# Where a vector engine reads its intermediate: halves of a product kept in PSUM instead of SBUF

## The chip, the cores and the metric

The kernel runs on one core of a Trainium2 chip. The metric is the device time of one execution in microseconds (us). Of the core's engines, TensorE (PE in the profile, PEld for its weight loads) multiplies matrices into PSUM, VectorE (DVE), ScalarE (ACT) and GpSimd (POOL) work on the results, and SyncE (SP) issues the DMAs between the chip's large memory (HBM) and the on-chip SBUF. The kernel uses PSUM as eight banks of 512 fp32 numbers per partition; TensorE's results go there, and GpSimd works on SBUF alone in this kernel. Each engine runs its own instructions in the order in which the program has them, and waits on semaphores for the others.

## The reference

Four batches of 12416 tokens with 128 channels pass through an attention over 32 inducing points, and every token's result through a gated feed-forward layer with 1536 hidden units:

```python
def mab(q, kv):
    s = scale * (q @ kv.transpose(0, 2, 1))
    s = s - s.max(-1, keepdims=True)
    a = np.exp(s)
    a /= a.sum(-1, keepdims=True) + 1e-09
    return a @ kv
h = mab(I, x)            # 32 points attend to all tokens of the batch
attn = mab(x, h)         # every token attends to the 32 points

g = attn @ w_gate
silu = g * (1.0 / (1.0 + np.exp(-g)))
val = attn @ w_val
out = (silu * val) @ w_out
```

x, the inducing points and the weights are fp32, and so is the output.

## The kernel before, in words

**Feed-forward.** The second attention is never multiplied out: gate and value weights are first multiplied by the batch's 32 points (st.w), and the tokens' attention weights (a stack of high and low halves) are the other operand. A batch is 25 *columns* of 512 or 480 tokens: one of 512 for the first blocks, then twelve of 512 and twelve of 480. Each column has 12 *tiles* of 128 hidden units. Batch 0 goes tile by tile in fp32r; batches 1 to 3 go by *pairs* of tiles in fp16, each fp32 number as a high half (its 16-bit cast) and a low half (the rest). A *slot* is one tile, so a column has 12 slots and a batch 300. For a pair the work is:

- fronts (L894): four matmuls, gate and value of two tiles, into two PSUM tiles gw of two banks each; three such tiles exist
- gates (L908): ScalarE makes silu of the gate, 2 x 512 or 2 x 480 numbers per partition
- values (L912): VectorE multiplies value, a factor and silu into h, in SBUF (5 buffers)
- splits, one pair later: h_hi is the cast of h to 16 bits (L916), h_lo = h - h_hi (L917). ScalarE casts, except tiles 6 and 7, which VectorE casts, and in batch 3 also tile 11; GpSimd subtracts, except tiles 2 and 3, which VectorE subtracts
- back (L934 to L936), 8 to 14 tiles later: three matmuls per tile, w_lo x h_hi, w_hi x h_hi and w_hi x h_lo, summed over the column's 12 tiles in one PSUM bank o; there are two such banks
- at the column's end VectorE scales o into SBUF (ob, L944), and a DMA writes it out

**Attention.** While batch b passes through the feed-forward layer, the attention of batch b + 1 is computed in small steps between its slots: scores (s1), two bursts of exp (e1 and e2), sums over tokens (hacc), the points and factors that scale them by powers of two (h_a to h_c, size_a to size_d), the tokens' scores (s2, s2_max, s2_sub), and the product with the weights (proj). The row sums and their reciprocals (sum2, rec2), normalization, transposes and halves (norm2, aT, a_hi, a_lo) follow during the batch itself, for four columns at a time. Steps that need a PSUM bank borrow the o bank that is not collecting a column.

**What sets the order.** The program is written out in order. plan() gives every attention step a slot, with numbers in PA (for batch 0) and PB (for batches 1 and 2); a step runs when the loop reaches its slot, but steps marked acc are held while the next back tile is 11, 0 or 1. Within a slot pair each engine gets, in this order, its part of fronts, gates and values of the new pair, splits of the pair before, backs, and attention steps. In batch 0, peak_of, peak_a, peak_b and peak_c find the largest weights, and half_a, half_b and half_c make the 16-bit halves of w_out; WPK and WOH are the slots where they start.

Of the kernel before, what the change touches and what calls it, by code (L numbers as in the profile page):

```python
# [110 lines left out]
@with_exitstack
def induced_set_attention_then_swiglu(ctx: ExitStack, tc: tile.TileContext, xt, xn, ind, wgv, wo, out):
# [104 lines left out]
    def peak_b():  # L217
        peaks = keep[-1]
        ps = ps_o.tile([P, 512], F32, name="o")
        for k in range(2):  # L220
# [4 lines left out]
        inverse2(top[:, 2:3], top[:, 1:2])

    def peak_c():
        nc.vector.tensor_scalar(out=top[:, 2:3], in0=top[:, 2:3], scalar1=2.0 ** TOP, scalar2=None, op0=ALU.mult)
# [73 lines left out]
    def attention(b, one, xn0=None, xt0=None):  # L302
# [209 lines left out]
        def size_b():
            ps = ps_o.tile([P, 512], F32, name="o")
            nc.tensor.matmul(out=ps[:, 0:M], lhsT=ones, rhs=st.size, start=True, stop=True)
# [15 lines left out]

# [76 lines left out]
        def rec2(q):  # L607
            nc.vector.reciprocal(out=st.sm[q][:, :FC[q]], in_=st.sm[q][:, :FC[q]])
            if st.half:
                nc.vector.tensor_mul(out=st.sm[q][:, :FC[q]], in0=st.sm[q][:, :FC[q]], in1=powers[:, 0:1].broadcast_to([P, FC[q]]))  # L610

# [285 lines left out]

    def on(u, two_, eng, call):

        if u.last or two_[0] != two_[1]:  # L900
            for k in range(2):
                call(eng[two_[k]], lambda x: x[:, k])
        else:
            call(eng[two_[0]], lambda x: x)

    def gates(u):
        u.s = twin(sip.tile([P, 2 * WF], F32, name="silu"), u)
        on(u, (0, 0), (nc.scalar,), lambda e, f: e.activation(out=f(u.s), in_=f(u.g), func=AF.Silu, scale=u.st.g))  # L908

    def values(u):  # L910
        u.h = twin(hp.tile([P, 2 * WF], F32, name="h"), u)
        on(u, (0, 0), (nc.vector,), lambda e, f: e.scalar_tensor_tensor(out=f(u.h), in0=f(u.v), scalar=u.st.k, in1=f(u.s), op0=ALU.mult, op1=ALU.mult))  # L912

    def splits(u):
        u.hi, u.lo = [twin(p.tile([P, WB], F32R, name=name).bitcast(F16)[:, :2 * WF], u) for p, name in ((hip, "h_hi"), (lop, "h_lo"))]
        on(u, [x.t in CAST2[u.b == B - 1] or u.cast_dve for x in u.us], (nc.scalar.copy, nc.vector.tensor_copy), lambda e, f: e(out=f(u.hi), in_=f(u.h)))  # L916
        on(u, [x.t in SUB2 or (u.last and x is u) for x in u.us], (nc.gpsimd, nc.vector), lambda e, f: e.tensor_sub(out=f(u.lo), in0=f(u.h), in1=f(u.hi)))  # L917
# [50 lines left out]
    for b in range(B):  # L968
        nxt = attention(b + 1, (one, oneb)[(b + 1) % 2]) if b + 1 < B else None
        if nxt is not None:  # L970
            nxt.steps = plan(nxt, PA if b == 0 else PB)
            if b == 0:
                cur.steps.append((nxt.e1, lambda: run(f"e2:52:{NTB}")))
                for q in range(2, NF):
                    base = NT * (1 + NG * (q - 1) - NST) + 2
# [2 lines left out]
                once = [lambda x=(k, i): peak_of(*x) for k in range(2) for i in range((6, 3)[k])] + [peak_a, lambda: None, peak_b, lambda: None, peak_c]
                peak_b.acc = (8, 9, 10, 11, 0, 1)
                cur.steps += [(WPK + 4 * i, f) for i, f in enumerate(once)]  # L980
                cur.steps += [(WOH + 4 * i, lambda i=i: (half_a, half_b, half_c)[i % 3](i // 3)) for i in range(9)]
# [95 lines left out]
```

## Time and profile before

| | us |
|---|---|
| median of 3 runs (lowest, highest) | 1488.93 (1487.92, 1491.02) |
| the profiled execution: time | 1488.93 |
| its span | 1487.2 |
| outside the span | 1.7 |

The mean granted TensorE clock was 0.995 of full speed. Column outputs (L944, and L946 in batch 0) begin where one column is summed up, so they cut the span: batch 0's last one begins at 421.70 us, batch 1's at 785.46, batch 2's at 1145.05, and batch 3's last but one at 1474.09.

A group line of the profile names the line, the engine, the operation, written and read tiles, shapes and the count, then busy us and the mean ns of one, then idle time before it and who ended it. A line of waits names who waited for whom, the total, the number and the longest. A line of the chain or of a timeline begins with the start and the duration. Durations of neighbours on one engine can overlap a little at their ends. In shapes, 128x960 and 128x2x480 are the same pair of 480-token tiles.

### The profile page before, as it was taken

To read this page: it belongs to the slowest core of one execution; us is meant where nothing else is said; L and a number is where in the kernel's file an instruction comes from. 1 tells how busy PE (TensorE), PEld (TensorE's weight loads), DVE (VectorE), ACT (ScalarE), POOL (GpSimd) and SP (SyncE) were. 2 spreads that over 40 slices of the span, in tenths; PEclk is the share of its full clock that TensorE was granted. 3 is DMA by queue.
4 is the path that set the end of the run, shared out by engine and by line. 5 is a ranking of instruction groups with operands and counts; after the bars stand their busy time and mean duration, and the time that the engine had idled before them with its cause. 6 is when DMAs were issued, how large, how long until landed. Compare 5 with 4: busy or idle time off the path is not lost.

```text
span 1487.2 us, 22279 instructions
## 1 busy us (share of the span) xinstructions
PE 1413.7 (95%) x7462; PEld 772.3 (52%) x7462; DVE 1276.4 (86%) x1572; ACT 1183.5 (80%) x1492; POOL 1175.7 (79%) x708
## 2 busy tenths in 40 slices
PE   8999999999999999999999998999999999999898
PEld 5677777788844443444444444344444344344443
DVE  6889878987888889688888887878888999999998
ACT  5887798799987876788888786688888787777786
POOL 1698769888978768688888776868888888888887
PEclk9999999999999999999999999999999999999999
DMA  9234422211124222110022431210001001000000
GB/s 369 64 99 154 141 72 94 104 48 48 43 91 164 80 101 96 37 39 29 30 81 78 172 101 47 100 43 31 30 29 34 29 26 32 22 32 31 28 24 26
DMA packets 50803, 107.75 MB, mean 72 GB/s; under 512 B 12928, under 2 KB 32896, under 8 KB 50688
## 3 DMA queue, kind: packets, MB, share of 16 engines
q1 hardware_dynamic: 50688, 106.33, 21.3%
q8 instruction: 59, 0.97, 0.3%
q14 instruction: 56, 0.46, 0.1%
HBM read 62.87 MB, written 25.43 MB: 59 GB/s over the span
## 4 chain that ended last, share of the span: by engine, by line
PE 63%; DVE 11%; ACT 10%; issue 6%; POOL 6%; DMA 3%; SPq 1%; POOLq 0%; DVEq 0%; ACTq 0%
PE gw L894 16%; PE o L936 12%; PE o L934 11%; PE o L935 11%; DVE h L912 6%; POOL h_lo L917 5%; ACT silu L908 5%; PE gv L854 4%; PE gv L853 4%; ACT h_hi L916 2%; ACT silu L859 1%; DVE h_lo L917 1%; PE o L436 1%; ACT h_hi L875 1%; DMA s_all<-wgv 1%
## 5 line engine op out<-in xcount | busy, mean ns | idle before, releaser
L917 POOL TENSOR_TENSOR h_lo<-h,h_hi 128x1024 f16<-128x1024 f32 (+1 forms) x375 | 796.9, 2147 | 204.5 <-ACT h_hi L916 84.2
L912 DVE SCALAR_TENSOR_TENSOR h<-gw,sc,silu 128x1024 f32<-128x1024 f32 (+1 forms) x451 | 558.0, 1241 | 122.3 <-ACT silu L908 108.1
L908 ACT ACTIVATE silu<-gw,sc 128x1024 f32<-128x1024 f32 (+1 forms) x451 | 489.8, 1087 | 181.5 <-PE gw L894 125.3
L916 ACT CAST h_hi<-h 128x1024 f16<-128x1024 f32 (+3 forms) x371 | 365.4, 985 | 36.5 <-DVE h L912 33.2
L936 PE MATMUL o<-h_lo,work 128*128 128x512 f16 (+1 forms) x900 | 336.7, 374 | 13.2 <-POOL h_lo L917 13.1
L935 PE MATMUL o<-h_hi,work 128*128 128x512 f16 (+1 forms) x900 | 337.0, 374 | 0.0
L934 PE MATMUL o<-h_hi,work 128*128 128x512 f16 (+1 forms) x900 | 336.7, 374 | 0.0
L894 PE MATMUL gw<-stack,work 128*128 128x512 f16 (+1 forms) x1200 | 302.0, 373 | 24.8 <-DVE h L912 19.0
L877 POOL TENSOR_TENSOR h_lo<-h,h_hi 128x512 fp32r<-128x512 f32 (+1 forms) x216 | 270.1, 1274 | 59.7 <-ACT h_hi L875 34.3
L894 PEld LDWEIGHTS <-work 128*128 128x128 f16 x1200 | 116.4, 98 | 170.6 <-issue 44.9
L859 ACT ACTIVATE silu<-gv 128x512 f32<-128x512 f32 (+1 forms) x300 | 176.3, 589 | 31.3 <-PE gv L853 24.8
L867 DVE TENSOR_TENSOR h<-gv,silu 128x512 f32<-128x512 f32 (+1 forms) x216 | 143.1, 667 | 38.3 <-ACT silu L859 24.5
L894 PE MATMUL gw<-stack,tw 128*128 128x512 f16 (+1 forms) x600 | 151.3, 374 | 9.9 <-DVE h L912 6.3
L934 PEld LDWEIGHTS <-work 128*128 128x128 f16 x900 | 88.4, 98 | 120.5 <-issue 24.2
L936 PEld LDWEIGHTS <-work 128*128 128x128 f16 x900 | 88.2, 98 | 101.1 <-issue 1.1
L935 PEld LDWEIGHTS <-work 128*128 128x128 f16 x900 | 88.1, 98 | 100.1 <-issue 1.0
L917 DVE TENSOR_TENSOR h_lo<-h,h_hi 128x1024 f16<-128x1024 f32 (+1 forms) x76 | 137.4, 1808 | 0.0
L875 ACT CAST h_hi<-h 128x512 fp32r<-128x512 f32 (+1 forms) x190 | 115.1, 606 | 14.9 <-DVE h L867 13.3
L853 PE MATMUL gv<-stack,tw 128*128 128x512 f32 (+1 forms) x300 | 120.5, 402 | 2.3 <-DVE stack L695 1.2
L854 PE MATMUL gv<-stack,tw 128*128 128x512 f32 (+1 forms) x300 | 117.0, 390 | 0.7 <-ACT silu L859 0.4
L934 PE MATMUL o<-h_hi,wo_lo 128*128 128x512 f32 (+1 forms) x288 | 112.8, 392 | 0.0
L935 PE MATMUL o<-h_hi,wo_hi 128*128 128x512 f32 (+1 forms) x288 | 111.4, 387 | 0.0
(216 smaller groups left out, 1386.3 us busy)
## 6 DMA issues: line engine op xcount, KB each, us to landing
xt_sb<-xt SPq DMA_DIRECT2D x32, 896.0 KB, 5.3
xn_sb<-xn SPq DMA_DIRECT2D x18, 896.0 KB, 6.7
out<-ob SPq DMA_DIRECT2D x52, 256.0 KB, 2.0
out<-ob SPq DMA_DIRECT2D x48, 240.0 KB, 2.0
xt_sb<-xt SPq DMA_DIRECT2D x4, 832.0 KB, 4.8
xn_sb<-xn SPq DMA_DIRECT2D x3, 832.0 KB, 4.6
stack<-a_hi SPq DMA_DIRECT2D x72, 32.0 KB, 1.8
stack<-a_lo SPq DMA_DIRECT2D x72, 32.0 KB, 1.9
```

The source lines that it names most:

```text
L853: nc.tensor.matmul(out=u.g[:, :n], lhsT=st.w[:, wcol(0, t)], rhs=rhs, start=True, stop=True)
L854: nc.tensor.matmul(out=u.v[:, :n], lhsT=st.w[:, wcol(1, t)], rhs=rhs, start=True, stop=True)
L859: nc.scalar.activation(out=u.s[:, :u.n], in_=u.g[:, :u.n], func=AF.Silu)
L877: eng.tensor_sub(out=u.lo[:, :n], in0=u.h[:, :n], in1=u.hi[:, :n].bitcast(F32))
L894: nc.tensor.matmul(out=x[:, 512 * (u.t - t):][:, :u.n], lhsT=st.w[:, wcol(k, u.t)], rhs=st.stack[c][:, :u.n], start=True, stop=True)
L908: on(u, (0, 0), (nc.scalar,), lambda e, f: e.activation(out=f(u.s), in_=f(u.g), func=AF.Silu, scale=u.st.g))
L912: on(u, (0, 0), (nc.vector,), lambda e, f: e.scalar_tensor_tensor(out=f(u.h), in0=f(u.v), scalar=u.st.k, in1=f(u.s), op0=ALU.mult, op1=ALU ...
L916: on(u, [x.t in CAST2[u.b == B - 1] or u.cast_dve for x in u.us], (nc.scalar.copy, nc.vector.tensor_copy), lambda e, f: e(out=f(u.hi), in_ ...
L917: on(u, [x.t in SUB2 or (u.last and x is u) for x in u.us], (nc.gpsimd, nc.vector), lambda e, f: e.tensor_sub(out=f(u.lo), in0=f(u.h), in1 ...
L934: nc.tensor.matmul(out=o[:, :n], lhsT=w_lo[:, ws], rhs=u.hi[:, :n], start=(t == 0), stop=False)
L935: nc.tensor.matmul(out=o[:, :n], lhsT=w_hi[:, ws], rhs=u.hi[:, :n], start=False, stop=False)
L936: nc.tensor.matmul(out=o[:, :n], lhsT=w_hi[:, ws], rhs=u.lo[:, :n], start=False, stop=(t == NT - 1))
```

## The change

Four things are changed.

1. **Owned pairs.** A pair can be *owned*: then its two tiles are handled apart. The product of the first goes to SBUF as before, and that of the second into the o bank that is not collecting (u.x). ScalarE casts and GpSimd subtracts the first half; VectorE casts and subtracts the second, from PSUM. A pair is owned when the next back tile is one of 1 to 6, no burst is due, no step marked acc is due within 5 slots or has run in the last 8, and the pair owned before lies at least two pairs back. The fixed choice of tiles (SUB2, CAST2) goes: pairs that are not owned are cast by ScalarE and subtracted by GpSimd. In a burst VectorE casts with a reduction over an axis of length one (one_wide). Of the 450 pairs 114 become owned: two per column in batch 3 (one in its last), two per column in most of batches 1 and 2, and one or none in columns 2 to 11 of these, where the next batch's attention runs.
2. **Small operations.** size_a takes absolute values with a reduction; size_b keeps its intermediates in PSUM; size_c, size_d and the factor in rec2 go from VectorE to ScalarE.
3. **Slots.** The size steps stand 2, 8, 12 and 16 slots after h_c instead of 2, 5, 8 and 11, and HB in PB begins 2 slots later.
4. **Batch 0.** The peak steps begin at slot 84, 3 apart (before: 66, 4 apart), with peak_a at 112, peak_b at 120 and the rest after the first burst; half_a to half_c begin at 216, 8 apart (before: 136, 4 apart), and their sum lies in an h buffer.

```diff
-SUB2, CAST2 = {2, 3}, ({6, 7}, {6, 7, 11})
-WPK, WOH = 66, 136
+OWN = range(1, 7)
+REST = 2
+WPK, WPA, WOH = 84, 112, 216
...
-PB = dict(... HB=(9, 3), ...)
+PB = dict(... HB=(11, 3), ...)
...
 def half_a(i):
-        joint[i] = sgl.tile([P, WF], F32, name="aT")
+        joint[i] = hp.tile([P, 2 * WF], F32, name="h")[:, :WF]
...
 def size_a():
-            nc.vector.tensor_scalar(out=st.size.bitcast(U32), in0=st.hT[:, 0:M].bitcast(U32), scalar1=0x7FFFFFFF, scalar2=None, op0=ALU.bitwise_and)
+            nc.vector.tensor_reduce(out=st.size, in_=st.hT[:, 0:M].unsqueeze(2), op=ALU.max, axis=AX.X, apply_absolute_value=True)
...
+        def grow(out, in_, by):
+            nc.scalar.activation(out=out, in_=in_, func=AF.Copy, scale=by)
+
 def size_c():
-            nc.vector.tensor_scalar(out=st.sc[:, 0:2], in0=powers[:, 0:2], scalar1=st.sc[:, 6:7], scalar2=None, op0=ALU.mult)
+            grow(st.sc[:, 0:2], powers[:, 0:2], st.sc[:, 6:7])
...
 def rec2(q):
-                nc.vector.tensor_mul(out=st.sm[q][:, :FC[q]], in0=st.sm[q][:, :FC[q]], in1=powers[:, 0:1].broadcast_to([P, FC[q]]))
+                nc.scalar.activation(out=st.sm[q][:, :FC[q]], in_=st.sm[q][:, :FC[q]], func=AF.Copy, scale=2.0 ** TOP)
...
-            add(hn + 3 * i + 2, step)
+            add(hn + (2, 8, 12, 16)[i], step)
...
+    halves = (lambda x: x[:, 0], lambda x: x[:, 1])
+    whole = (lambda x: x,)
...
 def values(u):
         u.h = twin(hp.tile([P, 2 * WF], F32, name="h"), u)
-        on(u, (0, 0), (nc.vector,), lambda e, f: e.scalar_tensor_tensor(out=f(u.h), in0=f(u.v), scalar=u.st.k, in1=f(u.s), op0=ALU.mult, op1=ALU.mult))
+        u.x = ps_o.tile([P, 512], F32, name="o")[:, :u.n] if u.own else None
+        u.parts = [(f, u.x if u.own and f is halves[1] else f(u.h)) for f in (halves if u.own else whole)]
+        for f, h in u.parts:
+            nc.vector.scalar_tensor_tensor(out=h, in0=f(u.v), scalar=u.st.k, in1=f(u.s), op0=ALU.mult, op1=ALU.mult)
+
+    def one_wide(out, in_):
+        nc.vector.tensor_reduce(out=out, in_=in_.unsqueeze(len(in_.shape)), op=ALU.max, axis=AX.X)

 def splits(u):
-        on(u, [x.t in CAST2[u.b == B - 1] or u.cast_dve for x in u.us], (nc.scalar.copy, nc.vector.tensor_copy), lambda e, f: e(out=f(u.hi), in_=f(u.h)))
-        on(u, [x.t in SUB2 or (u.last and x is u) for x in u.us], (nc.gpsimd, nc.vector), lambda e, f: e.tensor_sub(out=f(u.lo), in0=f(u.h), in1=f(u.hi)))
+        for f, h in u.parts:
+            (nc.vector.tensor_copy if h is u.x else one_wide if u.cast_dve else nc.scalar.copy)(out=f(u.hi), in_=h)
+        for f, h in u.parts:
+            (nc.vector if h is u.x else nc.gpsimd).tensor_sub(out=f(u.lo), in0=h, in1=f(u.hi))
...
+    quiet = {"own": 0, "step": 0}
+
+    def owned(slot, burst):
+
+        soon = [f for a in (cur, nxt) if a is not None for at, f in a.steps if at <= slot + 5]
+        ok = not burst and pend and pend[0].t in OWN and slot >= max(quiet.values()) and not any(hasattr(f, "acc") and f.acc for f in soon)
+        if ok:
+            quiet["own"] = slot + 2 * REST
+        return ok
...
+                cur.steps += [(WPK + 3 * i, f) for i, f in enumerate(once)]
+                cur.steps += [(WPA, peak_a), (WPA + 8, peak_b), (nxt.e1 + 9, peak_c), (nxt.e1 + 13, peak_d)]
+                cur.steps += [(WOH + 8 * i, lambda i=i: (half_a, half_b, half_c)[i % 3](i // 3)) for i in range(9)]
...
                 u.cast_dve = burst
+                u.own = u.last or owned(slot2, burst)
...
+                        if getattr(a.steps[0][1], "acc", ()):
+                            quiet["step"] = slot + 8
```

More of the change, by code (lines that the diff above doesn't have):

```diff
@@ L225, in peak_b, with peak_d @@
         inverse2(top[:, 2:3], top[:, 1:2])
-    def peak_c():
+    def peak_d():
         nc.vector.tensor_scalar(out=top[:, 2:3], in0=top[:, 2:3], scalar1=2.0 ** TOP, scalar2=None, op0=ALU.mult)
@@ L517, in size_b @@
             st.up, st.k, st.g, st.u, st.low = [c(i) for i in range(5)]
-            nc.vector.tensor_reduce(out=c(5), in_=ps[:, 0:M], op=ALU.max, axis=AX.X)
-            nc.vector.tensor_scalar(out=c(5), in0=c(5), scalar1=top[:, 0:1], scalar2=TINY, op0=ALU.mult, op1=ALU.max)
-            floor2(st.low, c(5))
+            nc.vector.tensor_reduce(out=ps[:, 64:65], in_=ps[:, 0:M], op=ALU.max, axis=AX.X)
+            nc.vector.tensor_scalar(out=ps[:, 65:66], in0=ps[:, 64:65], scalar1=top[:, 0:1], scalar2=TINY, op0=ALU.mult, op1=ALU.max)
+            floor2(st.low, ps[:, 65:66])
             inverse2(c(6), st.low)
+        def grow(out, in_, by):
+            nc.scalar.activation(out=out, in_=in_, func=AF.Copy, scale=by)
         def size_c():
-            nc.vector.tensor_scalar(out=st.sc[:, 0:2], in0=powers[:, 0:2], scalar1=st.sc[:, 6:7], scalar2=None, op0=ALU.mult)
-            nc.vector.tensor_scalar(out=st.sc[:, 2:4], in0=powers[:, 2:4], scalar1=st.low, scalar2=None, op0=ALU.mult)
-            nc.vector.tensor_mul(out=st.u, in0=st.u, in1=st.low)
+            grow(st.sc[:, 0:2], powers[:, 0:2], st.sc[:, 6:7])
+            grow(st.sc[:, 2:4], powers[:, 2:4], st.low)
+            grow(st.u, st.u, st.low)
         def size_d():
-            nc.vector.tensor_scalar(out=st.hT[:, 0:M], in0=st.hT[:, 0:M], scalar1=st.up, scalar2=None, op0=ALU.mult)
+            grow(st.hT[:, 0:M], st.hT[:, 0:M], st.up)
         def weights():
@@ L896, in fronts @@
         return u
[L898 to L904, printed above, removed]
+    halves = (lambda x: x[:, 0], lambda x: x[:, 1])
+    whole = (lambda x: x,)
     def gates(u):
         u.s = twin(sip.tile([P, 2 * WF], F32, name="silu"), u)
-        on(u, (0, 0), (nc.scalar,), lambda e, f: e.activation(out=f(u.s), in_=f(u.g), func=AF.Silu, scale=u.st.g))
+        for f in halves if u.last else whole:
+            nc.scalar.activation(out=f(u.s), in_=f(u.g), func=AF.Silu, scale=u.st.g)
     def values(u):
         u.h = twin(hp.tile([P, 2 * WF], F32, name="h"), u)
-        on(u, (0, 0), (nc.vector,), lambda e, f: e.scalar_tensor_tensor(out=f(u.h), in0=f(u.v), scalar=u.st.k, in1=f(u.s), op0=ALU.mult, op1=ALU.mult))
+        u.x = ps_o.tile([P, 512], F32, name="o")[:, :u.n] if u.own else None
[4 more added lines that the diff above has]
+        nc.vector.tensor_reduce(out=out, in_=in_.unsqueeze(len(in_.shape)), op=ALU.max, axis=AX.X)
     def splits(u):
         u.hi, u.lo = [twin(p.tile([P, WB], F32R, name=name).bitcast(F16)[:, :2 * WF], u) for p, name in ((hip, "h_hi"), (lop, "h_lo"))]
-        on(u, [x.t in CAST2[u.b == B - 1] or u.cast_dve for x in u.us], (nc.scalar.copy, nc.vector.tensor_copy), lambda e, f: e(out=f(u.hi), in_=f(u.h)))
-        on(u, [x.t in SUB2 or (u.last and x is u) for x in u.us], (nc.gpsimd, nc.vector), lambda e, f: e.tensor_sub(out=f(u.lo), in0=f(u.h), in1=f(u.hi)))
+        for f, h in u.parts:
+            (nc.vector.tensor_copy if h is u.x else one_wide if u.cast_dve else nc.scalar.copy)(out=f(u.hi), in_=h)
+        for f, h in u.parts:
+            (nc.vector if h is u.x else nc.gpsimd).tensor_sub(out=f(u.lo), in0=h, in1=f(u.hi))
         for k, x in enumerate(u.us):
@@ L977, in induced_set_attention_then_swiglu @@
                     cur.steps += post(cur, q, nc.gpsimd, base)
[L978 to L981, printed above, removed]
+                once = [lambda x=(k, i): peak_of(*x) for k in range(2) for i in range((6, 3)[k])]
+                cur.steps += [(WPK + 3 * i, f) for i, f in enumerate(once)]
+                cur.steps += [(WPA, peak_a), (WPA + 8, peak_b), (nxt.e1 + 9, peak_c), (nxt.e1 + 13, peak_d)]
+                peak_b.acc = (NT - 1, 0, 1)
+                cur.steps += [(WOH + 8 * i, lambda i=i: (half_a, half_b, half_c)[i % 3](i // 3)) for i in range(9)]
                 cur.steps.sort(key=lambda x: x[0])
@@ L1031, in induced_set_attention_then_swiglu @@
                     steps(slot)
+        quiet = {k: at - SLOTS for k, at in quiet.items()}
         if nxt is not None:
```

3 lines of the change are left out of this document (2 added, 1 removed).

## The prediction

> **What bounds the kernel now.** I read the page's busy line first, then the busy time in six stretches, then PE's pace in the chain of waits, then who waits for whom in batch 3.
>
> ```profile
> PE 1413.7 (95%) x7462; PEld 772.3 (52%) x7462; DVE 1276.4 (86%) x1572; ACT 1183.5 (80%) x1492; POOL 1175.7 (79%) x708
> ```
>
> 95% of PE says little here, because consecutive matmuls overlap in the records. The stretches below start and end at the start of a column's output copy (L944); they hold 11, 12, 11, 12, 12 and 11 columns. The columns are PE, PEld, DVE, ACT and POOL busy, clock, DMA share, GB/s.
>
> ```profile
> 441.14:614.17 173.03, 163.14 (x974) 72.06 (x972) 144.51 (x174) 128.99 (x127) 130.16 (x68) 0.99 0.29 100
> 614.17:768.58 154.41, 149.45 (x724) 70.59 (x723) 131.18 (x133) 129.27 (x133) 131.24 (x68) 1.00 0.11 34
> 800.28:977.12 176.84, 165.96 (x980) 73.66 (x979) 144.87 (x174) 129.63 (x128) 128.98 (x68) 0.98 0.29 98
> 977.12:1131.34 154.22, 149.18 (x723) 70.45 (x722) 131.29 (x133) 129.27 (x133) 131.36 (x68) 1.00 0.11 35
> 1158.82:1326.92 168.10, 157.46 (x715) 69.67 (x714) 159.96 (x139) 131.00 (x132) 138.20 (x66) 1.00 0.09 29
> 1326.92:1474.09 147.17, 137.93 (x668) 65.02 (x667) 139.83 (x123) 115.81 (x122) 122.73 (x61) 1.00 0.08 27
> ```
>
> Batch 3 (last two rows) is VectorE's: 160.0 of 168.1 us and 139.8 of 147.2 us, 95% in both, at 14.01 us for a 512-token column and 13.38 us for a 480-token one. The second halves of batches 1 and 2 take 12.87 and 12.85 us for the same 480 tokens, with VectorE at 85%. The chain shows what PE does when it waits for nothing: it passes one group of four gate and value matmuls (one pair of tiles) per period. First and last of five groups at 512 tokens, and of nine at 480:
>
> ```profile
> 1191.35 0.86 PE gw L894 x4
> ...
> 1199.99 0.86 PE gw L894 x4
> ```
> ```profile
> 657.92 0.81 PE gw L894 x4
> ...
> 674.12 0.81 PE gw L894 x4
> ```
>
> 8.64 us over 4 periods is 2.16 us a pair, and 16.20 over 8 is 2.025; six pairs make PE's own pace 12.95 us (512) and 12.15 us (480) a column. Above it lie 12.7 us in batch 3's 512-token columns (168.10 - 12 x 12.95), 13.5 us in its 480-token ones, 8.6 and 8.4 us in the second halves of batches 1 and 2. No more than these 43 us is to be had there. Who holds PE up in batch 3 (us in total, times, longest):
>
> ```profile
> PE gw L894 <- DVE h L912: 12.9, 12, 1.8
> PE o L936 <- POOL h_lo L917: 5.6, 11, 0.8
> ```
>
> And why VectorE is that full: VectorE, then GpSimd, in one column of batch 3.
>
> ```profile
> 1203.88 0.68 DVE L916 CAST h_hi<-h 128x1024 f16<-128x1024 f32 x1
> 1207.36 1.89 DVE L916 CAST h_hi<-h 128x512 f16<-128x512 f32 x1
> 1211.73 2.99 DVE L917 TENSOR_TENSOR h_lo<-h,h_hi 128x1024 f16<-128x1024 f32 x1
> ```
> ```profile
> 1204.73 4.23 POOL L917 TENSOR_TENSOR h_lo<-h,h_hi 128x1024 f16<-128x1024 f32 x2 [1.82 <-DVE h_hi L916]
> 1209.42 7.29 POOL L917 TENSOR_TENSOR h_lo<-h,h_hi 128x1024 f16<-128x1024 f32 x3 [0.46 <-DVE h_hi L916]
> ```
>
> A cast of half the size takes 1.89 us instead of 0.68. It starts while GpSimd subtracts and ends at 1209.25, 0.3 us behind GpSimd's pair (1208.96). The 2.99 us subtraction likewise lies inside GpSimd's next three, which take 7.29 us where the pair before took 2 x 2.12. With h in SBUF the two engines take turns. The Trainium skill (SBUF — State Buffer, "SBUF: two separate sides") has a rule for it: VectorE and GpSimd share one pair of ports, locked for a whole instruction, and the loser waits; these rows agree.
>
> **The change, part by part.** Prices, from groups of one line and shape (count, busy us, mean ns):
>
> ```profile
> L912 DVE SCALAR_TENSOR_TENSOR h<-gw,sc,silu 128x960 f32<-128x960 f32 x215 | 258.9, 1208 | 51.9 <-ACT silu L908 44.8 <-POOL h_lo L917 5.4
> L917 DVE TENSOR_TENSOR h_lo<-h,h_hi 128x960 f16<-128x960 f32 x36 | 66.9, 1859 | 0.0
> L916 DVE CAST h_hi<-h 128x960 f16<-128x960 f32 x36 | 31.1, 863 | 0.0
> L916 DVE CAST h_hi<-h 128x480 f16<-128x480 f32 x12 | 18.5, 1542 | 0.0
> L877 DVE TENSOR_TENSOR h_lo<-gv,h_hi 128x480 fp32r<-128x480 f32 x36 | 23.4, 649 | 0.1
> L867 DVE TENSOR_TENSOR gv<-gv,silu 128x480 f32<-128x480 f32 x36 | 23.8, 660 | 3.1 <-ACT silu L859 3.0
> L946 DVE COPY ob<-o 128x480 f32<-128x480 f32 x12 | 7.8, 647 | 0.0
> L917 POOL TENSOR_TENSOR h_lo<-h,h_hi 128x960 f16<-128x960 f32 x179 | 370.5, 2093 | 70.5 <-DVE h_hi L916 32.4 <-PE gw L894 17.0 <-ACT h_hi L916 14.8
> L877 POOL TENSOR_TENSOR h_lo<-h,h_hi 128x480 fp32r<-128x480 f32 x108 | 130.7, 1234 | 24.6 <-ACT h_hi L875 11.6 <-DVE h_hi L875 8.5 <-PE o L935 2.4
> L916 ACT CAST h_hi<-h 128x960 f16<-128x960 f32 x168 | 165.5, 985 | 16.6 <-DVE h L912 15.6
> L916 ACT CAST h_hi<-h 128x480 f16<-128x480 f32 x12 | 7.0, 584 | 0.7 <-DVE h L912 0.7
> ```
>
> The last two columns of the run hold the one half-size product and the last subtraction:
>
> ```profile
> L912 DVE SCALAR_TENSOR_TENSOR h<-gw,sc,silu 128x480 f32<-128x480 f32 x2 | 1.3, 703 | 0.0
> L917 DVE TENSOR_TENSOR h_lo<-h,h_hi 128x480 f16<-128x480 f32 x1 | 2.3, 2341 | 0.0
> ```
>
> *VectorE, batch 3, 480 tokens.* Out go one subtraction (1.86), one whole cast (0.86) and one half cast (1.54): 4.26 us. In come, for two owned pairs, two more product instructions (2 x 0.703 - 1.208 = 0.20 a pair), two casts from PSUM and two subtractions from PSUM. The subtraction from PSUM has its row, 0.65 (batch 0, where GpSimd is as busy). The product into PSUM has a relative, 0.66 in place in PSUM, beside 0.70 for a half in SBUF; I take 0.70. The cast from PSUM to 16 bits has none; it is nearest to the PSUM copy, 0.65, its ends being 0.43 (half of the SBUF cast's 0.863) and 1.54 (the half cast that waits). So 2 x (0.20 + 0.65 + 0.65) = 3.0 us in, and VectorE's 12.71 us a column (139.83/11) become 11.4. The skill has a rule against this (VectorE: DVE Perf Modes, "Why PSUM operands drop a tier"): an fp32 operand in PSUM loses the copy's double rate. By it the cast is 0.65; with the double rate it would be 0.43 and VectorE at 11.0.
>
> *ScalarE* gains half a cast in such a column: out 4 x 0.985 + 0.584, in 4 x 0.985 + 2 x 0.584, so 10.53 us (115.81/11) become 11.1. It also takes over a small multiplication behind the row sums, once in four columns, from VectorE:
>
> ```profile
> L610 DVE TENSOR_TENSOR sm<-sm,powers 128x15 f32<-128x15 f32 x9 | 11.5, 1273 | 0.3
> L294 DVE TENSOR_REDUCE pairs<-s_all 128x15 f32<-128x480 f32 x12 | 7.7, 643 | 0.0
> ```
>
> 1.27 us for 15 numbers a row, twice the reduction of 480, is again a wait for the port. On ScalarE it adds a wait instead: it follows the reciprocal, which stands behind a product (1.21) and that reduction (0.64), while ScalarE has only a cast (0.985) to do. So ScalarE stands still for some 1 us, 0.25 us a column, with the next pair's silu behind it and PE's next gate matmuls behind that. I put it inside the 0.25 that I add below. *GpSimd* gives one subtraction (2.09) for two halves between 1.05 and 1.23, I take 1.15: 11.16 becomes 11.4. All three then stand under PE's 12.15, at 91 to 94%, and none waits for a shared port. What is late next is PE itself. I add 0.25 us a column for what three engines at 94% still do to it (between 0 and the 0.72 that batch 1 shows): 12.4, and 13.2 at 512 tokens, where all scale alike.
>
> The order of VectorE's work in one 480-token column of batch 3, before, and then after (h, h_hi, h_lo: product, its 16-bit half, the rest; o: an output bank of PSUM):
>
> ```order
> L944 TENSOR_SCALAR ob<-o,sc 128x480
> L912 SCALAR_TENSOR_TENSOR h<-gw,sc,silu 128x2x480
> L916 CAST h_hi<-h 128x2x480
> L912 SCALAR_TENSOR_TENSOR h<-gw,sc,silu 128x2x480 x2
> L916 CAST h_hi<-h 128x480
> L912 SCALAR_TENSOR_TENSOR h<-gw,sc,silu 128x2x480 x2
> L917 TENSOR_TENSOR h_lo<-h,h_hi 128x2x480
> L912 SCALAR_TENSOR_TENSOR h<-gw,sc,silu 128x2x480
> ```
> ```order
> L954 TENSOR_SCALAR ob<-o,sc 128x480
> L917 SCALAR_TENSOR_TENSOR h<-gw,sc,silu 128x2x480
> L917 SCALAR_TENSOR_TENSOR h<-gw,sc,silu 128x480
> L917 SCALAR_TENSOR_TENSOR o<-gw,sc,silu 128x480
> L917 SCALAR_TENSOR_TENSOR h<-gw,sc,silu 128x2x480
> L925 CAST h_hi<-o 128x480
> L927 TENSOR_TENSOR h_lo<-o,h_hi 128x480
> L917 SCALAR_TENSOR_TENSOR h<-gw,sc,silu 128x480
> L917 SCALAR_TENSOR_TENSOR o<-gw,sc,silu 128x480
> ```
>
> No row of the second touches h in SBUF except to write it. The bank is read out one pair after it is taken, and it is taken only while the column's output stands between its tiles 1 and 6, so the next column's first output matmul finds it free and PE gains no wait. If not, PE waits for one subtraction, 0.65 us a column, as much as (b) below.
>
> *The sum.* Batch 3: 12 x (14.01 - 13.2) = 9.7 and 11 x (13.38 - 12.4) = 10.8. Its last pair loses a 2.34 us subtraction for one of 0.65: 1.5. Batches 1 and 2, second halves: 12 x 0.47 + 12 x 0.45 = 11.0.
>
> *Batches 1 and 2, columns 1 to 11,* hold the next batch's attention. From column 4 on hardly any pair is owned, so VectorE drops its cast and its subtraction, and each column gives GpSimd and ScalarE a sixth of both. PE's waits there in batch 1, and ScalarE's largest on GpSimd:
>
> ```profile
> PE gw L894 <- ACT silu L908: 2.4, 1, 2.4
> PE o L436 <- DMA xn_sb<-xn: 2.1, 1, 2.1
> PE o L363 <- DVE s_all L586: 1.8, 1, 1.8
> PE gw L894 <- DVE h L912: 1.3, 3, 0.6
> PE o L363 <- DVE s_all L398: 0.8, 1, 0.8
> PE o L514 <- DVE ob L944: 0.8, 1, 0.8
> ```
> ```profile
> ACT s_all L601 <- POOL s_all L598: 3.6, 1, 3.6
> ```
>
> The four of VectorE are 4.7 us; I take 3.5 as gained in each batch, 7. The DMA's wait stays, as the load it waits for moves by the same two slots as its reader. GpSimd's order up to the second exp, before and after (s_all<-s_all,mx: the maximum taken off the scores; the exp waits for the last of seven):
>
> ```order
> L203 TENSOR_TENSOR sc<-wide,sc 128x1
> L917 TENSOR_TENSOR h_lo<-h,h_hi 128x1024 x5
> L614 TENSOR_TENSOR s_all<-s_all,sm 128x480
> L917 TENSOR_TENSOR h_lo<-h,h_hi 128x1024 x2
> L598 TENSOR_TENSOR s_all<-s_all,mx2a 128x448
> ```
> ```order
> L204 TENSOR_TENSOR sc<-wide,sc 128x1
> L927 TENSOR_TENSOR h_lo<-h,h_hi 128x1024 x4
> L620 TENSOR_TENSOR s_all<-s_all,sm 128x480
> L927 TENSOR_TENSOR h_lo<-h,h_hi 128x1024 x3
> L604 TENSOR_TENSOR s_all<-s_all,mx2a 128x448
> ```
>
> The first row comes three slots later than before, so equal counts behind it mean one or two more subtractions ahead of the exp, up to 2 x 2.1 us. GpSimd loses its port waits in return. Ends: 14 us gained over both batches (all of VectorE's waits and ScalarE's 2.4), 8.6 lost. The small factors moved to ScalarE are hidden under its idle time. *Batch 0:* the weight peaks and the joined weights are only spread out, 1 us, between -4 and 4.
>
> 9.7 + 10.8 + 1.5 + 11.0 + 7 + 1 = 41 us, off the profiled execution's 1488.93 (span 1487.2), which is also the median: **1448 us**, with an own range of 1439 to 1460 (PE's pace plus 0.05 to plus 0.5 us in the 47 columns).
>
> **Rivals.** (a) *PE's pace, nothing left over.* If the shared port made all the waiting, columns run at 12.95 and 12.15: 12.7 + 13.5 + 1.5 + 17.0 + 7 + 1 = 53, 1436 us. The skill's lock rule would have it so. Against: three engines near 94% seldom fit without loss. (b) *ScalarE and GpSimd, in series, keep today's loss.* Batch 3 comes only to batch 1's 0.72 us above PE: 12 x 0.34 + 11 x 0.51 + 1.5 = 11 us, 1478. For: batch 1 loses 0.72 with VectorE at 85%. Against: it still has one locked subtraction a column. (c) *GpSimd late before the exp:* the 7 becomes -8.6, 1464. (d) *Slower: VectorE at PSUM is dearer than its rows.* If each owned pair costs e more, a 480-token column takes 11.4 + 2e on VectorE; it decides from e = 0.5, and at e = 1.0 batch 3 is where it was. At e = 1.3 (cast and subtraction doubled) it is 14.0: 11 x 0.6 + 12 x 0.9 + 24 x 1.1 = 44 us lost less 7, 1526. For: no row shows a 16-bit cast out of PSUM. Against: the 0.65 and 0.66 rows. (e) The columns don't move, 1488.
>
> **Chances.** Forecast 0.50, (a) 0.17, (b) 0.13, (c) 0.12, (d) 0.05, (e) 0.03. (a) to (c) and the forecast are faster: 0.92; within 0.2% (3 us, about what a measurement of this kernel tells from no change) 0.03; slower 0.05. The range 1433 to 1477 takes in (a), (c) and nearly (b).
>
> **What would show it.** Right: half casts and subtractions on VectorE near 0.65 us with no long tail, GpSimd's whole 512-token subtractions at 2.12 us with few above, batch 3 columns near 13.2 and 12.4, PE's wait on h under 4 us there. Wrong: PE waiting for GpSimd's h_lo instead, ScalarE waiting longer than 3.6 us before the second exp, or VectorE still at 95% of batch 3.

## The result, and the profile after

The changed kernel takes 1445.88 us (median; 1444.28 to 1446.7) against 1488.93 before: a ratio of 0.9707, 95% interval 0.9693 to 0.9721. The forecast was 1448. The profiled execution took 1444.72 us, its span 1442.9. The total is right; how it comes about is only half right, as the terms below show.

Busy time of the kernel after, from its page:

```profile
PE 1398.7 (97%) x7462; PEld 770.0 (53%) x7462; DVE 1184.9 (82%) x1704; ACT 1213.6 (84%) x1600; POOL 1186.1 (82%) x783
```

VectorE has 132 more instructions and 91.5 us less to do. The six stretches that the prediction showed of before, cut at the same columns (PE, PEld, DVE, ACT, POOL busy, clock, DMA share, GB/s). The cuts, there and here, lie 0.23 us ahead of the output starts that a timeline shows, all alike, so the lengths between them hold:

```profile
436.77:604.78 168.01, 160.92 (x974) 71.79 (x973) 124.45 (x158) 136.84 (x144) 142.02 (x78) 1.00 0.30 103
604.78:757.60 152.82, 148.33 (x725) 70.53 (x724) 131.56 (x177) 131.18 (x150) 129.50 (x81) 1.00 0.12 35
787.21:956.99 169.78, 161.96 (x979) 72.31 (x978) 124.55 (x158) 137.15 (x144) 141.93 (x77) 1.00 0.29 101
956.99:1109.81 152.82, 148.31 (x725) 70.54 (x724) 131.57 (x177) 131.10 (x150) 129.56 (x81) 1.00 0.12 35
1135.14:1294.37 159.23, 155.81 (x721) 70.23 (x720) 136.98 (x172) 136.64 (x148) 134.81 (x79) 1.00 0.10 30
1294.37:1431.19 136.82, 134.40 (x663) 64.48 (x662) 117.94 (x154) 119.40 (x135) 116.06 (x71) 1.00 0.09 29
```

Batch 3 is down from 168.10 to 159.23 and from 147.17 to 136.82, to 13.27 and 12.44 us a column (forecast 13.2 and 12.4), with all three engines at 85 to 87%. The second halves of batches 1 and 2 went from 154.41 and 154.22 only to 152.82 and 152.82, where 148.8 was forecast.

The prices, from groups of one line and shape (count, busy us, mean ns, idle before):

```profile
L917 DVE SCALAR_TENSOR_TENSOR o<-gw,sc,silu 128x480 f32<-128x480 f32 x72 | 51.6, 716 | 0.0
L925 DVE CAST h_hi<-o 128x480 f16<-128x480 f32 x72 | 46.6, 648 | 0.0
L927 DVE TENSOR_TENSOR h_lo<-o,h_hi 128x480 f16<-128x480 f32 x72 | 47.3, 658 | 2.5
L925 DVE CAST h_hi<-o 128x512 f16<-128x512 f32 x42 | 28.6, 680 | 0.0
L927 DVE TENSOR_TENSOR h_lo<-o,h_hi 128x512 f16<-128x512 f32 x42 | 29.0, 691 | 1.5
L927 POOL TENSOR_TENSOR h_lo<-h,h_hi 128x1024 f16<-128x1024 f32 x192 | 408.1, 2135 | 78.9 <-ACT h_hi L925 76.9
L927 POOL TENSOR_TENSOR h_lo<-h,h_hi 128x480 f16<-128x480 f32 x72 | 79.2, 1100 | 15.6 <-ACT h_hi L925 15.6
```

Cast and subtraction from PSUM take 0.65 and 0.66 us, as forecast, where a half cast from SBUF had taken 1.54 before. Who waits in batch 3 (us in total, times, longest):

```profile
ACT sm L616 <- DVE sm L614: 10.2, 5, 2.1
PE gw L900 <- ACT silu L910: 5.8, 5, 1.2
```

PE no longer waits for VectorE there (12.9 us before) nor for GpSimd (5.6). Its only wait there is new: five times, once per set of row sums, it waits for ScalarE's silu. Such a place, ScalarE, VectorE and PE in the timeline of one 480-token column of batch 3 (start, duration; the idle time before and its cause in brackets):

```profile
1351.28 0.98 ACT L925 CAST h_hi<-h 128x960 f16<-128x960 f32 x1
1354.28 0.21 ACT L616 ACTIVATE sm<-sm 128x15 f32<-128x15 f32 x1 [2.02 <-DVE sm L614]
1354.40 1.04 ACT L910 ACTIVATE silu<-gw,sc 128x960 f32<-128x960 f32 x1
```
```profile
1350.59 0.65 DVE L925 CAST h_hi<-o 128x480 f16<-128x480 f32 x1
1351.27 0.66 DVE L927 TENSOR_TENSOR h_lo<-o,h_hi 128x480 f16<-128x480 f32 x1
1351.85 0.71 DVE L917 SCALAR_TENSOR_TENSOR h<-gw,sc,silu 128x480 f32<-128x480 f32 x1
1352.47 0.72 DVE L917 SCALAR_TENSOR_TENSOR o<-gw,sc,silu 128x480 f32<-128x480 f32 x1
1353.10 0.64 DVE L297 TENSOR_REDUCE pairs<-s_all 128x15 f32<-128x480 f32 x1
1353.78 0.18 DVE L298 TENSOR_REDUCE sm<-pairs 128x15 f32<-128x30 f32 x1
1353.99 0.25 DVE L614 RECIPROCAL sm<-sm 128x15 f32<-128x15 f32 x1
```
```profile
1355.49 0.56 PE L900 MATMUL gw<-stack,work 128*128 128x480 f16 x2 [1.21 <-ACT silu L910]
```

ScalarE has cast a pair and stands for 2.02 us until VectorE has done these seven instructions, to multiply 15 numbers in 0.21 us; the silu behind that releases PE 1.21 us late. The starts of the column outputs show the loss:

```profile
1332.72 0.71 DVE L954 TENSOR_SCALAR ob<-o,sc 128x480 f32<-128x480 f32 x1
1344.87 0.71 DVE L954 TENSOR_SCALAR ob<-o,sc 128x480 f32<-128x480 f32 x1
1359.05 0.71 DVE L954 TENSOR_SCALAR ob<-o,sc 128x480 f32<-128x480 f32 x1
1370.68 0.71 DVE L954 TENSOR_SCALAR ob<-o,sc 128x480 f32<-128x480 f32 x1
```

A column without row sums takes 12.15 us, PE's pace. That with the row sums and the next, 14.18 + 11.63 = 25.81 us, are 1.51 over two at that pace (24.30).

### The profile page after: what moved, and what is told of

Same layout as the page of the kernel before. It is cut to its first block, busy times and chain, and to the rows that moved or that the text cites. A ratio compares the mean times of both kernels' runs of the same rounds, so it can differ in the third digit from the quotient of the medians.

```text
span 1442.9 us, 22347 instructions
## 1 busy us (share of the span) xinstructions
PE 1398.7 (97%) x7462; PEld 770.0 (53%) x7462; DVE 1184.9 (82%) x1704; ACT 1213.6 (84%) x1600; POOL 1186.1 (82%) x783
## 5 line engine op out<-in xcount | busy, mean ns | idle before, releaser
L927 POOL TENSOR_TENSOR h_lo<-h,h_hi 128x1024 f16<-128x1024 f32 (+2 forms) x450 | 821.4, 1840 | 154.2 <-ACT h_hi L925 151.2
L917 DVE SCALAR_TENSOR_TENSOR h<-gw,sc,silu 128x1024 f32<-128x1024 f32 (+2 forms) x450 | 502.1, 1117 | 163.8 <-ACT silu L910 151.6
L925 ACT CAST h_hi<-h 128x1024 f16<-128x1024 f32 (+3 forms) x446 | 404.3, 907 | 14.0 <-DVE h L917 13.4
L900 PE MATMUL gw<-stack,work 128*128 128x512 f16 (+1 forms) x1200 | 303.6, 373 | 18.1 <-ACT silu L910 16.5
L900 PE MATMUL gw<-stack,tw 128*128 128x512 f16 (+1 forms) x600 | 152.4, 373 | 10.6 <-ACT silu L910 9.6
L946 PE MATMUL o<-h_lo,wo_hi 128*128 128x512 f32 (+1 forms) x288 | 111.3, 387 | 0.1
```

The source lines that it names most:

```text
L900: nc.tensor.matmul(out=x[:, 512 * (u.t - t):][:, :u.n], lhsT=st.w[:, wcol(k, u.t)], rhs=st.stack[c][:, :u.n], start=True, stop=True)
L917: nc.vector.scalar_tensor_tensor(out=h, in0=f(u.v), scalar=u.st.k, in1=f(u.s), op0=ALU.mult, op1=ALU.mult)
L925: (nc.vector.tensor_copy if h is u.x else one_wide if u.cast_dve else nc.scalar.copy)(out=f(u.hi), in_=h)
L927: (nc.vector if h is u.x else nc.gpsimd).tensor_sub(out=f(u.lo), in0=h, in1=f(u.hi))
L946: nc.tensor.matmul(out=o[:, :n], lhsT=w_hi[:, ws], rhs=u.lo[:, :n], start=False, stop=(t == NT - 1))
```

## The experiments

Times are medians; ratios are to the kernel before, run beside each (1488.77 to 1489.05 us). "Stretch" means the six of above, in their order.

**The owned half back in SBUF.** The work stays the same, instruction for instruction; only the place of the second half differs.

```diff
-        u.x = ps_o.tile([P, 512], F32, name="o")[:, :u.n] if u.own else None
+        u.x = halves[1](u.h) if u.own else None
```

> The changed kernel with one thing undone: the second half of an owned pair stays in SBUF, in the upper half of its h tile. Engines, sizes and order are those of the changed kernel; only the place differs. Theory 'port' (VectorE and GpSimd take turns when VectorE reads h from SBUF, and that is where the time went): VectorE's half casts go from 0.65 us to about 1.5, its half subtractions from 0.66 to about 1.6, so each owned pair costs it some 1.8 us more; a 480-token column of batch 3 needs 11.0 + 3.6 = 14.6 us on VectorE instead of 12.4, and the whole 1490 to 1535 us, no better than before the change. Theory 'load' (the gain is that work was divided better among the engines): 1446 us, within 5.

1481.6 us, ratio 0.9949 (0.9932 to 0.9966): 36 of the 43 us are lost again by the place alone.

```profile
L925 DVE CAST h_hi<-h 128x480 f16<-128x480 f32 x72 | 71.0, 986 | 0.0
L927 DVE TENSOR_TENSOR h_lo<-h,h_hi 128x480 f16<-128x480 f32 x72 | 62.6, 870 | 2.5
L925 DVE CAST h_hi<-h 128x512 f16<-128x512 f32 x42 | 37.7, 899 | 0.0
L927 DVE TENSOR_TENSOR h_lo<-h,h_hi 128x512 f16<-128x512 f32 x42 | 43.6, 1038 | 1.4
```

```profile
PE gw L900 <- DVE h L917: 18.6, 36, 1.3
```

Against the rows from PSUM a 480-token pair costs VectorE 0.34 + 0.21 = 0.55 us more, and a 512-token one 0.22 + 0.35 = 0.57. That is less than the port's expectation asked, and the time is below its range (1490 to 1535 us), but 30 us and more above what the load theory allows. PE waits 18.6 us for VectorE's products, where the kernel after has 0.9. Columns of 480 tokens without row sums still run near 12.15. The loss sits where VectorE is fullest: column and next one with row sums, by output starts, 15.04 + 13.34 (1378.23, 1393.27, 1406.61) against 14.18 + 11.63. What holds the columns in the kernel after is a chain, not the sum of work. What the place costs once ScalarE's wait is out of that chain was not run.

**No pair owned but the last.** All casts go to ScalarE and all subtractions to GpSimd.

```diff
 def owned(slot, burst):
-        if ok:
-            quiet["own"] = slot + 2 * REST
-        return ok
+        return False
```

> The changed kernel with no owned pair but the last of the run: ScalarE casts and GpSimd subtracts everything, VectorE only makes products. Theory 'balance' (without VectorE's halves GpSimd sets the column): GpSimd needs 6 x 2.01 + 0.6 = 12.7 us in a 480-token column and 6 x 2.135 + 0.6 = 13.4 in a 512-token one, against 12.44 and 13.27 measured with owned pairs in batch 3; the whole 1450 to 1460 us. Rival 'keeping VectorE off SBUF was all, the owned halves do nothing': 1446 us, within 3.

1439.41 us, 0.9665 (0.965 to 0.9679): 6.5 us *faster* than with the owned pairs. Both expectations missed it: balance had 1450 to 1460 us, its rival 1446.

```profile
PE 1399.8 (97%) x7462; PEld 770.9 (54%) x7462; DVE 1045.4 (73%) x1365; ACT 1254.7 (87%) x1600; POOL 1285.4 (89%) x783
ACT sm L616 <- DVE sm L614: 28.1, 19, 1.9
PE gw L900 <- ACT silu L910: 18.1, 21, 1.9
```

In the kernel after, the same two waits are 34.3 us in 19 and 26.1 us in 27. In batch 3 ScalarE stands 1.5 to 1.6 us for a reciprocal here and 2.0 to 2.1 there: without its casts and subtractions VectorE reaches the reciprocal sooner. In the kernel after, then, the halves in PSUM were not what made the gain: it is enough that VectorE leaves the casts and subtractions to ScalarE and GpSimd, and GpSimd at 89% keeps up.

**ScalarE's multiplication one pair later.** The reciprocal stays where it is; its multiplication by a power of two moves one slot further, into the next pair's steps.

```diff
         def rec2(q):
             nc.vector.reciprocal(out=st.sm[q][:, :FC[q]], in_=st.sm[q][:, :FC[q]])
+
+        def scale2(q):
             if st.half:
                 nc.scalar.activation(out=st.sm[q][:, :FC[q]], ..., scale=2.0 ** TOP)
...
-        steps = [..., (1, lambda: f["rec2"](q)), (2, lambda: f["norm2"](q, eng)),
+        steps = [..., (1, lambda: f["rec2"](q)), (2, lambda: f["scale2"](q)), (2, lambda: f["norm2"](q, eng)),
```

> The changed kernel with ScalarE's multiplication of the reciprocal row sums written one pair later, behind that pair's silu and cast and ahead of the normalization; nothing else. Theory 'ScalarE waits': ScalarE stands up to 2.1 us for the reciprocal (34.3 us in 19 waits), the next silu and PE's next gate matmuls stand behind it, and this is the 1.4 to 1.5 us by which every fourth column is longer than PE's pace; with it gone these columns come to 12.15 and 12.95 us, some 18 times 1.4 us, so 1421 to 1428 us. Rival 'VectorE's row sums themselves (1.07 us between two products) hold the products up': 1446 us, within 3.

1421.01 us, 0.954 (0.9526 to 0.9555): 25 us off the kernel after, where PE waited 26.1 us for silu; 20 us of that wait are gone.

```profile
PE gw L904 <- ACT silu L914: 5.9, 8, 1.9
```
```profile
1332.20 0.21 ACT L620 ACTIVATE sm<-sm 128x15 f32<-128x15 f32 x1 [0.38 <-DVE sm L614]
```
```profile
1322.79 0.71 DVE L958 TENSOR_SCALAR ob<-o,sc 128x480 f32<-128x480 f32 x1
1335.54 0.71 DVE L958 TENSOR_SCALAR ob<-o,sc 128x480 f32<-128x480 f32 x1
1347.16 0.71 DVE L958 TENSOR_SCALAR ob<-o,sc 128x480 f32<-128x480 f32 x1
```

ScalarE's wait at such a place falls from 2.02 to 0.38 us, and the pair of columns takes 12.75 + 11.62 us, 0.07 over PE's pace.

**The same multiplication on VectorE,** as before the change; all else as after.

```diff
-                nc.scalar.activation(out=st.sm[q][:, :FC[q]], ..., func=AF.Copy, scale=2.0 ** TOP)
+                nc.vector.tensor_mul(out=st.sm[q][:, :FC[q]], ..., in1=powers[:, 0:1].broadcast_to([P, FC[q]]))
```

> The changed kernel with one thing undone: the factor in rec2 is multiplied on VectorE again (tensor_mul with two SBUF operands), as before the change. Theory 'ScalarE's in-order wait is the 1.4 us a set of row sums': VectorE's multiplication costs 0.4 us (mean of the run with the owned pairs alone) instead of 1.27 before, since VectorE and GpSimd seldom want the port at once now, and ScalarE waits for nothing; the pairs of columns with row sums come from 25.8 to 24.7 us (480 tokens): 1446 - 18 x 1.1 = 1426 us, 4 or more above the run with the late multiplication (1421). Rival 'the other small factors or the size slots cost it': 1440 us or more.

1425.34 us, 0.9572 (0.9558 to 0.9586), as forecast: moving this one operation to ScalarE cost 20.5 us.

```profile
L616 DVE TENSOR_TENSOR sm<-sm,powers 128x15 f32<-128x15 f32 x9 | 2.7, 295 | 0.3
```

The 1.27 us that had spoken for moving it are 0.30 here (for 16 numbers 1.23 and 0.47). The owned pairs alone bring it down as well, in the next run: to 0.38 and 0.44. So the owned pairs had already cured it.

**Owned pairs alone:** the kernel before with owned() and the code that it needs (the new values and splits, without SUB2 and CAST2) and the reduction as cast in bursts (one_wide), but its own small operations, slots and batch 0.

```diff
-SUB2, CAST2 = {2, 3}, ({6, 7}, {6, 7, 11})
+OWN = range(1, 7)
+REST = 2
```

> The kernel before with the owned pairs alone (and the reduction as cast in bursts): small factors on VectorE, the old slots of the size steps, HB 9, and batch 0's old slots. By the terms measured between the two traces, batch 0 (4.4 us) and the shorter wait for xn (3.2 us) are lost, and the small factors cost about as much on VectorE as on ScalarE: 1453 to 1458 us. Rival 'the small changes carry half of the gain': 1465 us or more.

1437.84 us, 0.9659 (0.9642 to 0.9675), below the range. So changes 2 to 4 together cost 8 us, and the owned pairs by themselves bring 51.

```profile
1132.93:1288.59 155.66, 155.50 (x721) 70.42 (x720) 137.33 (x175) 136.88 (x145) 135.12 (x79) 1.00 0.10 31
1288.59:1423.12 134.53, 134.14 (x663) 64.61 (x662) 118.17 (x156) 119.48 (x133) 115.88 (x71) 1.00 0.09 29
```

Batch 3 at 12.97 and 12.23 us a column, PE's pace (12.95, 12.15) within 0.1, with the engines as full as in the kernel after.

**The late multiplication, and no pair owned:** the edits of both.

> The late multiplication (1421 us) with no owned pair but the last of the run. With ScalarE's wait gone this asks again whether VectorE's halves are worth anything. Theory 'balance': GpSimd needs 6 x 1.98 + 0.75 = 12.6 us a 480-token column with the attention rows' work spread over four, against 12.3 measured with halves, so 0.2 to 0.3 us a column over 47 columns: 1430 to 1436 us. Rival 'halves are worth nothing': 1421 us, within 3. Third: without VectorE's halves the row sums start sooner: below 1418.

1427.41 us, 0.9581 (0.9563 to 0.96): 6.4 us slower than with owned pairs (1421.01). With ScalarE's wait gone the owned pairs are worth something after all, less than the balance expectation asked.

```profile
PE gw L904 <- DVE h L921: 9.0, 12, 2.3
DVE aT L628 <- POOL s_all L624: 21.5, 17, 3.8
```

PE's largest wait is on VectorE's product again, 9.0 us against 1.2 in the run with owned pairs. VectorE in turn stands for GpSimd's normalization, ahead of the transpose that needs it and the product behind that: 21.5 us here against 2.6 with owned pairs. So it is GpSimd's load, as the balance expectation had it, but by way of the attention's rows.

**Before, with its two sets of tiles emptied:** VectorE casts only in bursts and subtracts only in the last pair; nothing goes to PSUM.

```diff
-SUB2, CAST2 = {2, 3}, ({6, 7}, {6, 7, 11})
+SUB2, CAST2 = set(), (set(), set())
```

> The kernel before with two sets emptied, SUB2 and CAST2, and nothing else: ScalarE casts and GpSimd subtracts every pair except the last subtraction and the casts in bursts. No PSUM halves, no moved step. Theory 'keeping VectorE off h in SBUF is the whole gain': as the run without owned pairs (1439), less ScalarE's wait (about 0.5 us a set of row sums in that run's columns, 18 of them), plus batch 0 and the wait for xn (3 and 3 us): 1433 to 1440 us. Theory 'the halves in PSUM are needed': 1460 us or more.

1464.63 us, 0.9834 (0.981 to 0.9858): some 25 us above the first theory's range, and as the second had it. The group of the multiplication in rec2, and one of its instructions beside GpSimd and PE:

```profile
L610 DVE TENSOR_TENSOR sm<-sm,powers 128x15 f32<-128x15 f32 x9 | 17.3, 1927 | 0.3
```
```profile
795.68 5.58 DVE L610 TENSOR_TENSOR sm<-sm,powers 128x16 f32<-128x16 f32 x1
```
```profile
788.65 12.57 POOL L917 TENSOR_TENSOR h_lo<-h,h_hi 128x1024 f16<-128x1024 f32 x6
```
```profile
802.50 1.75 PE L894 MATMUL gw<-stack,tw 128*128 128x512 f16 x4 [4.50 <-DVE h L912]
```

A multiplication of 16 numbers starts at 795.68 and ends at 801.26; GpSimd's six subtractions end at 801.22. PE then waits 4.50 us for the product behind it. With GpSimd that full, VectorE's last small multiplication in SBUF waits until three of them have ended, and PE behind it. Six waits of PE behind such multiplications sum to 17 us. Against the run with the owned pairs alone, 1464.63 - 1437.84 = 27 us, so most of the difference is this: with owned pairs GpSimd is busy for 83% of the span, here for 88%, and the multiplication finds gaps. That run also casts in bursts by the reduction (one_wide), so the 27 us are not the owned pairs' alone:

```profile
L916 DVE CAST h_hi<-h 128x1024 f16<-128x1024 f32 x4 | 15.2, 3788 | 0.1
```

Two of these four casts took 6.56 and 6.57 us, where the reduction took 1.22. By the output starts, the two columns around them lose little by it: 0.4 us in batch 1 and 2.0 in batch 2.

**HB back at 9,** all else as after.

```diff
-PB = dict(... HB=(11, 3), ...)
+PB = dict(... HB=(9, 3), ...)
```

> The changed kernel with HB in PB back at 9: in batches 1 and 2 the sums over tokens and what follows stand 2 slots earlier again. Theory 'the reader moved, the load did not': the last load of xn is issued behind the column's output and four stack DMAs in SP's queue wherever its slot is, so PE's wait for xn comes back to 2.1 and 2.8 us (0.2 and 1.5 with HB 11), and column 7 of batches 1 and 2 becomes 2 us or more longer. Rival 'as the prediction had it, load and reader move together': PE's wait for xn stays at 0.2 and 1.5 us, and the shorter column 7 comes from the size steps.

A single execution: 1448.0 us beside 1489.02, 2 us above the median of the kernel after and not to be told from it. What its trace shows is the wait. PE's in this kernel, and in the one after:

```profile
PE o L439 <- DMA xn_sb<-xn: 4.4, 2, 2.5
```
```profile
PE o L439 <- DMA xn_sb<-xn: 1.7, 2, 1.5
```

The last load's issue on SP's queue, again in this kernel and in the one after:

```profile
529.43 0.53 SPq L349 DMA_DIRECT2D xn_sb<-xn  x1
```
```profile
529.60 0.53 SPq L349 DMA_DIRECT2D xn_sb<-xn  x1
```

The slot moves the reader, not the load: on SP's queue the load stands behind the column's output and four stack transfers, and issues at the same time in both. Column 7 of batches 1 and 2 is 2.3 and 3.2 us longer than in the kernel after, as expected.

**Late multiplication, and the halves of w_out in their old slots.**

```diff
-WPK, WPA, WOH = 84, 112, 216
+WPK, WPA, WOH = 84, 112, 136
...
-        joint[i] = hp.tile([P, 2 * WF], F32, name="h")[:, :WF]
+        joint[i] = sgl.tile([P, WF], F32, name="aT")
...
-                cur.steps += [(WOH + 8 * i, ...) for i in range(9)]
+                cur.steps += [(WOH + 4 * i, ...) for i in range(9)]
```

> The late multiplication (1421 us) with the 16-bit halves of w_out at their old slots (136, 4 apart) and their sum in its old tile. In batch 0 columns 18 to 24 took 95.6 us with the new slots and 92.3 with the old ones, columns 11 to 13 took 47.0 with the new and 49.2 with the old. Theory 'these steps cost the same wherever they stand': 1420 us, within 2. Rival 'columns 11 to 13 gained by the peak steps, not by these': 1417 to 1418 us.

1418.35 us, 0.9524 (0.9508 to 0.9539), the lowest time of all. Its interval overlaps that of the late multiplication alone. In the traces batch 0's last output starts at 414.94 us instead of 416.10, so nothing here shows a gain from the new slots of half_a to half_c. Columns 11 to 13 of batch 0 take 47.6 us, against 49.2 before and 47.0 with the late multiplication alone: that gain does not come from these slots. It may come from the peak steps, which no run moves alone.

## Why the prediction came out right, and where it did not

Microseconds gained over before, by stretches between output starts; the first column is the prediction's, the others are measured.

| term | predicted | after | owned pairs alone | after, multiplication on VectorE |
|---|---|---|---|---|
| batch 3, 512 tokens | 9.7 | 8.9 | 12.4 | 12.4 |
| batch 3, 480 tokens | 10.8 | 10.3 | 12.6 | 12.6 |
| last pair | 1.5 | 1.4 | 1.3 | 1.4 |
| second halves of batches 1 and 2 | 11.0 | 3.0 | 12.4 | 10.4 |
| columns 1 to 11 of batches 1 and 2 | 7 | 12.1 | 8.0 | 18.1 |
| batch 0 | 1 | 4.4 | 1.4 | 5.0 |
| columns 24 and 0 between batches | not named | 4.2 | 4.2 | 4.2 |
| span | 41 | 44.3 | 52.3 | 64.2 |

**Right:** what bounded the kernel and why. VectorE and GpSimd took turns in SBUF, and reading from PSUM ends it: putting the half back costs 36 us with no other edit. Giving the work to the other engines ends it too (1439.41 us with no owned pair), which the prediction did not set up as a rival. VectorE's prices hold within 0.02 us (product into PSUM 0.70 taken, 0.716 measured; cast 0.65, 0.648; subtraction 0.65, 0.658), and GpSimd's half within 0.05 (1.15 taken, 1.10 and 1.16 measured), so rival (d) falls. With the halves in SBUF its e is 0.55, just past the 0.5 from which it was to decide, and 36 of the 43 us are gone, though in the columns with row sums and not by VectorE's sum, as (d) has it: 10.7 + 2 x 0.55 = 11.8 us is still under PE's 12.15. PE hardly waits for the borrowed bank: 0.3 us once, and 1.7 and 1.9 us in all in the runs with the owned pairs alone and with the multiplication on VectorE. Rival (b) falls, with batch 3 at 0.32 and 0.29 us above PE's pace instead of 0.72, and so does (c). ScalarE's longest wait before the second exp is 3.2 us against 3.6:

```profile
ACT s_all L607 <- POOL s_all L604: 3.2, 1, 3.2
```

The marks under "what would show it" came as written. Two sums of the prediction are off, neither by enough to matter: the last pair's rows give 2.34 - 0.65 = 1.7 us, not 1.5, and rival (b) leaves out the 7 and 1 us that the others count.

**The step that failed is the 0.25 us a column,** "for what three engines at 94% still do" to PE, with ScalarE's stand of "some 1 us" inside it. At the loads that came, three busy engines cost PE next to nothing: with owned pairs alone the residual in batch 3 is 0.02 and 0.08 us a column at the same busy times, which is rival (a). That rival had 0.17, and the argument against it, that three such engines seldom fit without loss, did not hold here. Nor were the engines as full as reckoned. A 480-token column takes 10.7 us of VectorE, 10.9 of ScalarE and 10.6 of GpSimd, 87 to 89% of PE's pace and not 91 to 94%. VectorE's subtraction, taken out at its mean of 1.86 us, had cost 2.21 in that stretch, the multiplication that moves to ScalarE (0.36 us a column) was not taken out at all, and GpSimd's whole pairs fell from 2.14 to 2.01. What engines at 94% would cost PE stays open. The stand of ScalarE, in turn, was counted too low. It was reckoned from one product and one reduction on VectorE against ScalarE's cast. It left out that the cast and the subtraction which the change itself puts on VectorE (0.65 and 0.66) stand ahead of the reciprocal, and the second reduction and the reciprocal (0.18 and 0.25) behind it. With no owned pair, when only the latter are there, ScalarE still stands 1.5 us at the same places. In the kernel after it stood 2.02 us and PE 1.21 of it at such a place, 20.5 us in all by the runs. Batch 3's 0.25 was about right (0.32 and 0.29 measured) for the wrong reason; the second halves of batches 1 and 2 were expected to gain more than half of what stood above PE's pace, and since the same wait stands there at four sets of row sums in each, they gave 3.0 of 11.0.

**Attention columns, 7 against 12.1, and batch 0, 1 against 4.4.** "The DMA's wait stays, as the load it waits for moves by the same two slots as its reader" is wrong: the load stays behind SP's other transfers and the reader moves past it. PE's waits of 2.1 and 2.8 us before are 0.2 and 1.5 after. The rest of changes 2 to 4, without rec2, is worth 18.1 - 8.0 = 10 us in these columns, of which that wait explains some 3; which of the other edits brought the remainder was not taken apart. In batch 0 a wait of PE on the peak steps is gone, which the prediction had overlooked; it is 2.35 us of the 4.4, and the rest was not taken apart. Of the kernel before:

```profile
181.77 0.41 PE L412 MATMUL o<-mm,fold 128*128 128x28 f32 x2 [2.35 <-DVE top L222]
```

**What was not forecast:** 4.2 us in columns 24 and 0, where a batch changes. They come with the owned pairs alone, and 3.9 of them with the two sets merely emptied, so they don't need the halves in PSUM; columns 24 of batches 1 and 2 and 0 of the next fall by 2.1 us each time.

So the total is near because errors offset each other. Without ScalarE's wait (last column of the table) the change would have brought 64 us, 23 more than forecast: 8 in the columns without attention (3.8 in those of the sum, 4.2 where a batch changes), 15 in the attention columns and batch 0. The wait took 20 of it back.

## What to carry to other kernels

An operation moved to an engine with idle time still has to be placed: price it by what it waits for and by what stands behind it in that engine's order, not by its own length; 21 multiplications of at most 16 numbers a row cost 20 us here, and nothing that shows when written one pair later. Where two engines hold each other up through SBUF, count every operand that goes through the shared place, small ones too, and test changes of one package together and apart, since the value of one (the owned pairs: -6.5, 6 and up to 27 us) depends on the others.

## What the hardware showed beyond that

The wait of a small VectorE instruction behind GpSimd has no fixed size. The multiplication of 15 or 16 numbers (three times of 4) occurs 21 times in the kernel before with its two sets emptied. Once GpSimd had just paused, and it took 0.17 us; 14 times it ended with the GpSimd instruction in progress (0.3 to 1.1 us); five times it was passed over once more (3.3 to 3.6 us), and once twice, the 5.58 us of above. In the six long cases GpSimd stopped only because its own next instruction, the normalization, waits for these numbers. The casts of 6.56 and 6.57 us in the same kernel are alike: one that ran freely in the kernel before took 0.68, and here GpSimd went on until its next subtraction needed the cast. What decides who goes first between two GpSimd instructions stays open.

The reciprocals of 15 or 16 numbers, with one operand in SBUF, took 0.24 to 0.26 us in every kernel. In the kernel after, casts and subtractions from PSUM varied by less than 3% over 114 pairs (casts of 480 numbers: 0.644 to 0.658 us).
